# Lightning attention and a mish MLP on one core: attention outputs and scores on parts of the TensorE array

## The chip, the cores and the metric

The kernel runs on one core of a Trainium2 chip. The metric is the device time of one execution in microseconds (us); three runs of the kernel before gave a median of 219.52 us (219.44 to 220.08). A core has TensorE for matmuls (PE in the profile, its weight loads PEld), VectorE (DVE), ScalarE (ACT), GpSimd (POOL) and SyncE (SP), which issues transfers. TensorE reads its operands from SBUF and writes only to PSUM, a small memory of eight banks; VectorE and ScalarE bring results from there back to SBUF.

## The reference

Inputs are q, k, v of shape (4, 8, 768, 64), a decay lam per head, and the weights w_in (512, 2048) and w_out (2048, 512). Attention is linear attention with decay, in blocks along the sequence:

```python
for b in range(nb):
    intra = einsum('bhic,bhjc->bhij', qb, kb) * Dmask      # lam ** (i - j), i >= j
    intra = einsum('bhij,bhjd->bhid', intra, vb)
    inter = einsum('bhid,bhde->bhie', qb * lam_pow, kv_state)
    out[:, :, sl] = intra + inter
    kv_state = lam_block * kv_state + einsum('bhsd,bhse->bhde', kb_dec, vb)
```

The heads are then laid side by side, x of shape (3072, 512), and pass through an MLP: h = x @ w_in, g = h * tanh(softplus(h)), output g @ w_out in float32.

## The kernel before, in words

The sequence is cut into NG = 6 groups of C = 128 positions, n = 0 to 5 in the code (the first to the sixth group); a group holds these positions of all four batches, 512 tokens. For a group n, attention writes a transposed tile xt (features on partitions, tokens along the row). The first product of the MLP (mm1_unit, line 427) makes 16 blocks of 128 features of 512 tokens, each of four 128x512 matmuls, and ScalarE applies mish into hsg (line 434). The second product is a plain one for n = 0 (mm2_unit) and, in the others, a scheme of seven products with sums of weights and tokens (fast_unit, line 593), 14 units of eight matmuls of 256 columns (line 525), whose token sums gsum VectorE makes (line 498).

Attention of group n+1 is woven into the units of group n. In this text, stage n is the time in which the units of group n run. The work of a group's attention is cut into eight half-heads: a batch b and four of the eight heads (hf), that is two pairs of heads. Each half-head has three pieces, and att_pieces (line 397) lists them as att_a of half-head t, att_s of t-1, att_o of t-2. The loop over units at the end takes one or two pieces behind each unit, by a table (room). Each engine works its own queue in the order in which the program gives it the instructions.

- att_a (line 306): in the third to the sixth group (n >= NT = 2) q and k come already transposed by DMA, issued by SyncE in turn (line 263): qraw and kraw, k scaled by its decay on GpSimd or VectorE first (ktil, line 259). TensorE updates the state with att_kv (line 276: two 128-column matmuls of ktil and v into pv). VectorE multiplies qraw by its decay (qT, line 318) and copies kraw into kz (line 322): kz holds for each pair a tile in which only the 64 rows of one head are filled and the other 64 are zero, so that a matmul over all 128 rows gives one head's scores. VectorE adds state and pv (raw, line 298), GpSimd multiplies by the block decay (w, line 299). In the second group (n = 1) TensorE does the transposes and ScalarE fills kz (line 344).
- att_s (line 353): four 128x128 matmuls per half-head, kz stationary, qT moving, into one PSUM bank psS; from n = 2 on two banks, named pS and pk, are used in turn by successive half-heads. VectorE multiplies 512 columns by the causal mask into sb (line 362).
- att_o (line 365): for each pair, a matmul of the state w (128x128, the two heads as diagonal blocks) with qT, then two matmuls with sb, whose stationary operand is v in vz: a tile in which 64 columns of v alternate with 64 zero columns, so that 128 columns that start at a head's v give that head on the first 64 partitions and zero on the others, and 128 that start at the zeros ahead of the next head's v give that head on the last 64; the three matmuls of a pair accumulate in psO. ScalarE copies to xt (line 382).

The first group (n = 0) has no state and is done ahead of the loop: first_t transposes, first_s computes scores per head from 64 rows of the array, with the two heads of a pair in two banks (line 230), first_o the outputs with vz (line 244). TensorE is kept busy there with matmuls of zeros (busy, line 162). All loads of q, k, v, w_in (win) and w_out are issued by GpSimd; v goes into vz (line 80). vz has eight buffers and kz four; their zeros are written once by VectorE (lines 152, 700, 702).

Of the kernel before, what the change touches and what calls it, by code (L numbers as in the profile page):

```python
# [7 lines left out]
F32 = mybir.dt.float32  # L8
F16 = mybir.dt.float16
AF = mybir.ActivationFunctionType  # L10
ALU = mybir.AluOpType


def bc(ap, axis, n):
    shape = list(ap.shape)
    shape.insert(axis, n)
    return ap.unsqueeze(axis).broadcast_to(shape)
# [3 lines left out]
def kernel(  # L21
# [10 lines left out]
    nc = tc.nc  # L32
    B, H, S, D = q.shape
    C = 128
# [8 lines left out]
    NVB = 8  # L43
    NKB = 4
    NT = 2

    ctx.enter_context(tc.manual_schedule())
    const = ctx.enter_context(tc.tile_pool(name="const", bufs=1))
    loads = ctx.enter_context(tc.tile_pool(name="loads", bufs=NVB))
    work = ctx.enter_context(tc.tile_pool(name="work", bufs=2))  # L50
# [3 lines left out]
    kn = [None] * (NG * B)  # L54
    qn = [None] * (NG * B)

    vz = [const.tile([128, H, 2 * D], F16, name=f"vz{i}") for i in range(NVB)]

    def chunk_rows(t, i):
        n, b = divmod(i, B)  # L60
        return t[b, :, n * C : (n + 1) * C, :].rearrange("h p c -> p h c")
# [15 lines left out]
        nc.gpsimd.dma_start(out=qn[i], in_=chunk_rows(q, i))  # L77

    def load_v(i):
        nc.gpsimd.dma_start(out=vz[i % NVB][:, :, 0:D], in_=chunk_rows(v, i))  # L80

    WS = 4

# [64 lines left out]
    kzero = kzero2[:, 0:128]  # L148
    one1 = const.tile([1, 128], F32, name="one1")
    nc.vector.memset(one1, 1.0)  # L150
    for i in range(B):
        nc.vector.memset(vz[i][:, :, D : 2 * D], 0.0)
    kz = [const.tile([128, 2, 2, C], F16, name=f"kz{i}") for i in range(NKB)]
    nc.vector.tensor_scalar(out=ident, in0=rel, scalar1=0.0, scalar2=None, op0=ALU.is_equal)
    nc.vector.tensor_scalar(out=gone, in0=rel, scalar1=0.0, scalar2=-30000.0,
# [48 lines left out]
    sb0 = {}  # L204
# [31 lines left out]
    def first_o(c):  # L236
        if xt[0] is None:
            xt[0] = work.tile([128, JP, GT], F16, name="xt", tag="xt", bufs=2)
        psO = ps.tile([128, JP, C], F32, name="pO", tag="pO")
        vf = vz[c].rearrange("p h c -> p (h c)")  # L240
        for j in range(JP):
            for t in range(2):
                o = 4 * D * j + D * t
                nc.tensor.matmul(psO[:, j, :], vf[:, o : o + 128], sb0[c][t][:, j, :],
                                 start=(t == 0), stop=(t == 1))
        nc.scalar.activation(xt[0][:, :, c * C : (c + 1) * C], psO, AF.Copy)


# [27 lines left out]
    def att_kv(s, spare):  # L276

        n, b, hf = s.n, s.b, s.hf
        i = n * B + b
        pv = ps.tile([128, 2, 128], F32, name="pv", tag=spare, bufs=2)  # L280
        for p in range(2):
            j = 2 * hf + p
            nc.tensor.matmul(  # L283
                pv[:, p, :].rearrange("p (a e) -> p a e", a=2),
                ktil[i][:, 4 * hf + 2 * p : 4 * hf + 2 * p + 2, :].rearrange("p h c -> p (h c)"),
                vz[i % NVB][:, 2 * j : 2 * j + 2, 0:D], start=True, stop=True,
            )
        s.pv = pv

# [16 lines left out]
    def att_a(s):  # L306

        n, b, hf = s.n, s.b, s.hf
        i = n * B + b
        lqh = lq[:, 2 * hf : 2 * hf + 2, :]  # L310
        s.qT = work.tile([128, 2, C], F16, name="qT", tag="qT", bufs=5)
        s.kz = kz[s.seq % NKB]
        kp = [ktil[i][:, 4 * hf + 2 * p : 4 * hf + 2 * p + 2, :].rearrange("p h c -> p (h c)")
              for p in range(2)]
        if n >= NT:
            if n < NG - 1:
                att_kv(s, s.spare)
            nc.vector.tensor_tensor(  # L318
                out=s.qT, in0=qraw[i][:, 2 * hf : 2 * hf + 2, :], in1=lqh, op=ALU.mult)
            for hp in range(2):  # L320
                rs = slice(64 * hp, 64 * hp + 64)
                nc.vector.tensor_copy(s.kz[rs, :, hp, :], kraw[i][rs, 2 * hf : 2 * hf + 2, :])  # L322
            if n < NG - 1:
                att_w(s)
            if hf == 0 and i + 2 < s.loaded:
                turn(i + 2)
            if hf == 1 and i + B < NG * B:
                load_chunk(i + B)
            return
        pk = ps.tile([128, 2, C], F32, name="pk", tag="pk")  # L330
        pq = ps.tile([128, 2, C], F16, name="pq", tag="pq")
        for p in range(2):
            nc.tensor.matmul(pk[:, p, :], kp[p], ident, start=True, stop=True)
        for p in range(2):
            j = 2 * hf + p
            nc.tensor.matmul(
                pq[:, p, :], qn[i][:, 2 * j : 2 * j + 2, :].rearrange("p h c -> p (h c)"),
                ident, is_transpose=True, start=(p == 0), stop=(p == 1),
            )
        att_kv(s, s.spare)  # L340
        nc.vector.tensor_tensor(out=s.qT, in0=pq, in1=lqh, op=ALU.mult)
        for hp in range(2):
            rs = slice(64 * hp, 64 * hp + 64)
            nc.scalar.activation(s.kz[rs, :, hp, :], pk[rs], AF.Copy)
        if hf == 0 and i + 1 < s.loaded:
            scale_k(i + 1)
        elif hf == 0:
            turn(i + 1)
        att_w(s)
        if hf == 1:  # L350
            ahead.pop(0)()

    def att_s(s):

        psS = ps.tile([128, 4, C], F32, name="pS", tag=("pS", "pk")[s.seq % 2 if s.n >= NT else 0])
        for p in range(2):
            for hp in range(2):
                nc.tensor.matmul(  # L358
                    psS[:, 2 * p + hp, :], s.kz[:, p, hp, :], s.qT[:, p, :], start=True, stop=True,
                )  # L360
        s.sb = work.tile([128, 4, C], F16, name="sb", tag="sb", bufs=4)
        nc.vector.tensor_tensor(  # L362
            out=s.sb, in0=psS, in1=bc(maskT, 1, 4), op=ALU.mult)

    def att_o(s):

        n, b, hf = s.n, s.b, s.hf
        i = n * B + b
        if xt[n] is None:
            xt[n] = work.tile([128, JP, GT], F16, name="xt", tag="xt", bufs=2)  # L370
        psO = ps.tile([128, 2, C], F32, name="pO", tag=("pO", "pq")[s.seq % 2 if s.n >= NT else 0])
        vf = vz[i % NVB].rearrange("p h c -> p (h c)")
        for p in range(2):
            j = 2 * hf + p
            nc.tensor.matmul(psO[:, p, :], wst[b][hf][n % 2][:, p, :], s.qT[:, p, :],
                             start=True, stop=False)
            for hp in range(2):
                o = 4 * D * j + D * hp
                nc.tensor.matmul(psO[:, p, :], vf[:, o : o + 128], s.sb[:, 2 * p + hp, :],  # L379
                                 start=False, stop=(hp == 1))  # L380
        dst = xt[n][:, 2 * hf : 2 * hf + 2, b * C : (b + 1) * C]
        nc.scalar.activation(dst, psO, AF.Copy)  # L382

# [261 lines left out]
    for n in range(NG):  # L645
# [31 lines left out]
        for u, (fn, args) in enumerate(units):  # L677
            rest = fn(*args)
            if n == 0 and 19 <= u < 23:
                weight_sum(0 if u < 21 else 2, u % 2)  # L680
            if n == 1 and 4 <= u < 8:
                weight_sum(1 if u < 6 else 3, u % 2)
            if n > 0 and u in (9, 10):
                token_sum(n, 2, u - 9)
            if n > 0 and u == NKI - 3:
                token_sum(n, 0, 0)
            if n > 0 and u == NKI - 2:
                token_sum(n, 1, 0)
            if n > 0 and u == NKI - 1:
                token_sum(n, 0, 1)  # L690
                token_sum(n, 1, 1)
            if n > 0 and u in (NKI + 2, NKI + 3):
                token_sum(n, 3, u - NKI - 2)
            if n == 0 and 2 <= u < 2 + nh:
                att_kv(first_halves[u - 2], "po")
                att_w(first_halves[u - 2])
            if n == 0 and u % 2 == 1 and 0 < (u + 1) // 2 < B:
                scale_k((u + 1) // 2)
            if n == 0 and nh + 2 <= u < nh + 2 + NVB - B:
                nc.vector.memset(vz[u - nh - 2 + B][:, :, D : 2 * D], 0.0)  # L700
            if n == 0 and nh + 2 <= u < nh + 2 + NKB:
                nc.vector.memset(kz[u - nh - 2], 0.0)
            if n == 0 and u == 17:
                q_decays()
            if n == 0 and u == 16:
                nc.vector.tensor_scalar(out=maskT, in0=rel, scalar1=0.0, scalar2=None, op0=ALU.is_ge)
            if n == 0 and u == 18:
                scale_k(B)
            if n > 0 and pieces and u == 0:
                if n > 1:  # L710
                    turn((n + 1) * B)
                turn((n + 1) * B + 1)
            for _ in range(room.get(u, 0)):
                f2, s = pieces.pop(0)
                s.spare = "po" if u < NKI - 1 else "ph"
                f2(s)
            if n == 0 and rest:
                rest()
# [34 lines left out]
```

## Time and profile before

The profiled execution has a span of 217.4 us from its first to its last instruction; its own time is not among the three runs, whose median, 219.52 us, stands 2.1 us above that span.

| | before |
|---|---|
| median of 3 runs | 219.52 us (219.44 to 220.08) |
| span of the profiled execution | 217.4 us |
| TensorE busy | 204.8 us, 1672 matmuls |
| VectorE busy | 146.1 us, 309 instructions |
| ScalarE busy | 101.3 us |
| GpSimd busy | 116.6 us |
| granted TensorE clock | 1.000 |

A row of the profile names the line of the kernel, the engine, the operation, output and inputs, shapes and count; in the grouped view it then gives busy us in all, mean ns of one, the idle time before them, and what ended it. In the timeline a row begins with start and length in us, and a bracket at its end gives the engine's idle time just before and what released it. Matmuls are pipelined: one of 128 columns is shown with 0.22 us, though the next follows after about 0.055 us.

### The profile page before, as it was taken

How to read it: one execution, taken by the hardware profiler on the slowest of the kernel's cores; microseconds unless marked ns; L12 is line 12 of the kernel's file. 1: busy time of each engine (PE TensorE's matmuls, PEld its weight loads, DVE VectorE, ACT ScalarE, POOL GpSimd, SP SyncE). 2: the span in 40 equal slices, each digit the busy share in tenths (PEclk: the TensorE clock that was granted, in tenths of full speed). 3: DMA queues.
4: the chain of work that ended last, by engine and by line, in shares of the span. 5: the costliest groups of instructions: out<-in, count | busy, mean ns of one | idle time of the engine just before them, and what ended most of it. 6: DMA issues, size and time to landing. Idle time of an engine off the chain costs nothing.

```text
span 217.4 us, 4272 instructions
## 1 busy us (share of the span) xinstructions
PE 204.8 (94%) x1672; PEld 136.6 (63%) x1672; DVE 146.1 (67%) x309; ACT 101.3 (47%) x190; POOL 116.6 (54%) x139
## 2 busy tenths in 40 slices
PE   7899999999999799999979999979999999999993
PEld 2465544576545587745669845669845699644893
DVE  6667561877669999339999419999439987213433
ACT  5465566567665231166522176623166632266410
POOL 7996334998988768808757908757700002000020
PEclk9999999999999999999999999999999999999999
DMA  9999999999999999975999965999985201300014
GB/s 133 141 158 198 203 203 175 175 152 125 150 149 104 100 75 121 163 152 70 104 71 113 142 160 74 119 75 71 151 168 100 48 3 48 130 18 0 0 59 137
DMA packets 103766, 24.66 MB, mean 113 GB/s; under 512 B 93890, under 2 KB 103234, under 8 KB 103746
## 3 DMA queue, kind: packets, MB, share of 16 engines
q0 software_dynamic: 78080, 13.37, 80.3%
q1 hardware_dynamic: 22688, 8.39, 17.8%
q10 hardware_dynamic: 2978, 2.62, 4.0%
q8 instruction: 13, 0.21, 0.4%
q14 instruction: 7, 0.06, 0.1%
HBM read 27.26 MB, written 6.29 MB: 154 GB/s over the span
## 4 chain that ended last, share of the span: by engine, by line
PE 63%; DVE 20%; POOL 5%; issue 4%; DMA 4%; ACT 1%; ACTq 0%; POOLq 0%; DVEq 0%
PE ph L420 26%; PE z L525 10%; PE po L442 6%; PE y L525 6%; PE x L525 5%; DVE qT L318 5%; DVE kz L322 4%; DVE sb L362 4%; DVE gsum L498 4%; DMA win<-in_moe_w_in_dram 4%; PE pO L379 3%; DVE raw L298 3%; PE pS L358 2%; PE fin L525 2%; POOL vz L80 2%
## 5 line engine op out<-in xcount | busy, mean ns | idle before, releaser
L420 PE MATMUL ph<-xt,win 128*128 128x512 f16 (+2 forms) x404 | 89.6, 368 | 0.5 <-ACT hsg L434 0.2
L434 ACT ACTIVATE hsg<-ph 128x512 f16<-128x512 f32 x96 | 57.0, 597 | 45.6 <-PE ph L420 45.5
L420 PEld LDWEIGHTS <-win 128*128 128x128 f16 x404 | 37.0, 98 | 35.1 <-issue 0.6
L299 POOL TENSOR_TENSOR w<-raw,lbm 128x256 f16<-128x256 f32 x32 | 25.2, 791 | 29.0 <-DVE raw L298 28.9
L578 POOL TENSOR_TENSOR u<-u,p 128x512 f32<-128x512 f32 x5 | 6.5, 1293 | 52.0 <-DVE u L576 52.0
L525 PEld LDWEIGHTS <-gsum 128*128 128x128 f16 x336 | 30.8, 98 | 3.5 <-issue 0.5
L362 DVE TENSOR_TENSOR sb<-pS,maskT 128x512 f16<-128x512 f32 x40 | 27.2, 683 | 2.0 <-PE pS L358 1.9
L382 ACT ACTIVATE xt<-pO 128x256 f16<-128x256 f32 x40 | 15.2, 382 | 27.4 <-PE pO L379 27.2
L318 DVE TENSOR_TENSOR qT<-qraw,lq 128x256 f16<-128x256 f16 x32 | 19.1, 598 | 10.3 <-DMA qraw<-qn 10.3
L525 PEld LDWEIGHTS <-hsg 128*128 128x128 f16 x240 | 22.7, 98 | 2.5
L69 POOL DMA_DIRECT2D kn<-in_k_dram x23 | 21.4, 932 | 4.5 <-DMA win<-in_moe_w_in_dram 1.7
L80 POOL DMA_DIRECT2D vz<-in_v_dram x24 | 21.7, 906 | 3.3 <-DMA wout<-in_moe_w_out_dram 1.7
L77 POOL DMA_DIRECT2D qn<-in_q_dram x23 | 20.7, 898 | 5.1 <-DMA wout<-in_moe_w_out_dram 3.3
L498 DVE TENSOR_TENSOR gsum<-hsg 128x1024 f16<-128x1024 f16 x20 | 14.5, 725 | 12.9 <-ACT hsg L434 12.9
L322 DVE COPY kz<-kraw 64x256 f16<-64x256 f16 x64 | 19.9, 311 | 1.9 <-DMA kraw<-ktil 0.9
L379 PE MATMUL pO<-sb,vz 128*128 128x128 f16 x160 | 17.3, 219 | 3.6 <-DVE sb L362 3.2
L525 PE MATMUL z<-tsum,gsum 128*128 128x256 f16 x160 | 20.4, 272 | 0.2
L525 PE MATMUL x<-wout,hsg 128*128 128x256 f16 x160 | 20.1, 273 | 0.0
L358 PE MATMUL pS<-qT,kz 128*128 128x128 f16 x160 | 16.6, 220 | 1.8 <-DVE kz L322 1.6
L358 PEld LDWEIGHTS <-kz 128*128 128x128 f16 x160 | 11.8, 98 | 7.8 <-DVE kz L322 3.0
L298 DVE TENSOR_TENSOR raw<-pv,w 128x256 f32<-128x256 f32 x32 | 13.5, 422 | 4.1 <-PE pv L283 3.4
L379 PEld LDWEIGHTS <-vz 128*128 128x128 f16 x160 | 12.6, 98 | 5.7 <-issue 4.9
(89 smaller groups left out, 242.8 us busy)
## 6 DMA issues: line engine op xcount, KB each, us to landing
out_dram<-osum SPq DMA_DIRECT2D x14, 256.0 KB, 3.2
vz<-in_v_dram POOLq DMA_DIRECT2D x24, 128.0 KB, 4.7
kn<-in_k_dram POOLq DMA_DIRECT2D x23, 128.0 KB, 4.4
qn<-in_q_dram POOLq DMA_DIRECT2D x23, 128.0 KB, 4.6
wout<-in_moe_w_out_dram POOLq DMA_DIRECT2D x4, 512.0 KB, 16.5
win<-in_moe_w_in_dram POOLq DMA_DIRECT2D x3, 512.0 KB, 10.1
out_dram<-osum ACTq DMA_DIRECT2D x5, 256.0 KB, 4.0
out_dram<-osb ACTq DMA_DIRECT2D x4, 256.0 KB, 5.5
```

What stands on the lines that cost most here:

```text
L69: nc.gpsimd.dma_start(out=kn[i], in_=chunk_rows(k, i))
L80: nc.gpsimd.dma_start(out=vz[i % NVB][:, :, 0:D], in_=chunk_rows(v, i))
L299: nc.gpsimd.tensor_tensor(out=w_new, in0=raw, in1=lb, op=ALU.mult)
L318: nc.vector.tensor_tensor(out=s.qT, in0=qraw[i][:, 2 * hf : 2 * hf + 2, :], in1=lqh, op=ALU.mult)
L322: nc.vector.tensor_copy(s.kz[rs, :, hp, :], kraw[i][rs, 2 * hf : 2 * hf + 2, :])
L358: nc.tensor.matmul(psS[:, 2 * p + hp, :], s.kz[:, p, hp, :], s.qT[:, p, :], start=True, stop=True,)
L362: nc.vector.tensor_tensor(out=s.sb, in0=psS, in1=bc(maskT, 1, 4), op=ALU.mult)
L379: nc.tensor.matmul(psO[:, p, :], vf[:, o : o + 128], s.sb[:, 2 * p + hp, :], start=False, stop=(hp == 1))
L420: nc.tensor.matmul(ph_t[ni][:, lo:hi], win0[min(ni, 2)][:, kc, max(ni - 2, 0) * 128 : max(ni - 2, 0) * 128 + 128] if ni < w else win[ni // ...
L434: nc.scalar.activation(hsg[n][:, ni, :], ph_t.pop(ni), AF.Mish)
L498: nc.vector.tensor_tensor(out=gsum[n, i][:, ks, :], in0=a, in1=b, op=op)
L525: nc.tensor.matmul(t, lhs(kk, b), rhs(kk, c, c + w), start=(fresh and kk == 0 and (alone or i == 0)), stop=(kk == HK - 1), skip_group_chec ...
```

## The change

v is loaded without zero columns (vd in place of vz). In the outputs of all groups each head's matmul with sb has 64 stationary columns and writes its own 64 partitions of psO; the two heads of a pair differ in the half of the array's columns that they use. The state matmuls keep 128 columns and now both come first. In the groups n = 2 to 5 the scores are taken from kraw itself: 64 rows of it and of qT for each head, one head of a pair into the bank pS and the other into pk, and the mask is multiplied in two operations of 256 columns, one for each bank. The copies into kz go in these groups (they stay for n = 1), and so do the memsets of vz.

```diff
-    vz = [const.tile([128, H, 2 * D], F16, name=f"vz{i}") for i in range(NVB)]
+    vd = [const.tile([128, H, D], F16, name=f"vd{i}") for i in range(NVB)]
...
-        nc.gpsimd.dma_start(out=vz[i % NVB][:, :, 0:D], in_=chunk_rows(v, i))
+        nc.gpsimd.dma_start(out=vd[i % NVB], in_=chunk_rows(v, i))
...
-    for i in range(B):
-        nc.vector.memset(vz[i][:, :, D : 2 * D], 0.0)
...
-        vf = vz[c].rearrange("p h c -> p (h c)")
         for j in range(JP):
             for t in range(2):
-                o = 4 * D * j + D * t
-                nc.tensor.matmul(psO[:, j, :], vf[:, o : o + 128], sb0[c][t][:, j, :],
-                                 start=(t == 0), stop=(t == 1))
+                nc.tensor.matmul(psO[64 * t : 64 * t + 64, j, :], vd[c][:, 2 * j + t, :],
+                                 sb0[c][t][:, j, :], start=True, stop=True)
...
-                vz[i % NVB][:, 2 * j : 2 * j + 2, 0:D], start=True, stop=True,
+                vd[i % NVB][:, 2 * j : 2 * j + 2, :], start=True, stop=True,
...
-            for hp in range(2):
-                rs = slice(64 * hp, 64 * hp + 64)
-                nc.vector.tensor_copy(s.kz[rs, :, hp, :], kraw[i][rs, 2 * hf : 2 * hf + 2, :])
...
-        psS = ps.tile([128, 4, C], F32, name="pS", tag=("pS", "pk")[s.seq % 2 if s.n >= NT else 0])
+        if s.n >= NT:
+            i = s.n * B + s.b
+            t = [ps.tile([128, 2, C], F32, name="pS", tag=tag) for tag in ("pS", "pk")]
+            for p in range(2):
+                for hp in range(2):
+                    rs = slice(64 * hp, 64 * hp + 64)
+                    nc.tensor.matmul(t[hp][:, p, :], kraw[i][rs, 2 * s.hf + p, :], s.qT[rs, p, :],
+                                     start=True, stop=True)
+            s.sb = work.tile([128, 2, 2, C], F16, name="sb", tag="sb", bufs=4)
+            for hp in range(2):
+                nc.vector.tensor_tensor(
+                    out=s.sb[:, hp], in0=t[hp], in1=bc(maskT, 1, 2), op=ALU.mult)
+            return
+        psS = ps.tile([128, 4, C], F32, name="pS", tag="pS")
...
-        vf = vz[i % NVB].rearrange("p h c -> p (h c)")
         for p in range(2):
-            j = 2 * hf + p
             nc.tensor.matmul(psO[:, p, :], wst[b][hf][n % 2][:, p, :], s.qT[:, p, :],
-                             start=True, stop=False)
+                             start=(p == 0), stop=False, skip_group_check=True)
+        for p in range(2):
             for hp in range(2):
-                o = 4 * D * j + D * hp
-                nc.tensor.matmul(psO[:, p, :], vf[:, o : o + 128], s.sb[:, 2 * p + hp, :],
-                                 start=False, stop=(hp == 1))
+                nc.tensor.matmul(psO[64 * hp : 64 * hp + 64, p, :],
+                                 vd[i % NVB][:, 4 * hf + 2 * p + hp, :],
+                                 s.sb[:, hp, p, :] if n >= NT else s.sb[:, 2 * p + hp, :],
+                                 start=False, stop=True, skip_group_check=True)
...
-            if n == 0 and nh + 2 <= u < nh + 2 + NVB - B:
-                nc.vector.memset(vz[u - nh - 2 + B][:, :, D : 2 * D], 0.0)
```

## The prediction

> **What bounds the kernel now.** I read the page first, then busy time by stretch, then the chain of waits and single stretches of the timeline.
>
> ```profile
> span 217.4 us, 4272 instructions
> ...
> PE 204.8 (94%) x1672; PEld 136.6 (63%) x1672; DVE 146.1 (67%) x309; ACT 101.3 (47%) x190; POOL 116.6 (54%) x139
> ...
> PE 63%; DVE 20%; POOL 5%; issue 4%; DMA 4%; ACT 1%; ACTq 0%; POOLq 0%; DVEq 0%
> ```
>
> TensorE is busy nearly all the time and carries 63% of the chain that ended last, yet VectorE carries 20%. To see where, I cut the span at the group borders. Stage n works on the MLP of group n and on the attention of group n+1; the rows are stages 1 to 4 (start, end and length, then busy us of each engine with its instructions).
>
> ```profile
> core 0: us, PE busy (x) PEld busy (x) DVE busy (x) ACT busy (x) POOL busy (x), PEclk, DMA share, GB/s
> 57.00:90.60 33.60, 30.96 (x261) 21.68 (x261) 26.41 (x52) 13.22 (x26) 27.93 (x32) 1.00 1.49 115
> 90.60:124.00 33.40, 31.98 (x274) 22.65 (x272) 25.52 (x52) 14.21 (x27) 22.20 (x27) 1.00 1.05 112
> 124.00:157.40 33.40, 31.97 (x274) 22.65 (x272) 25.54 (x52) 14.21 (x27) 21.15 (x24) 1.00 1.04 111
> 157.40:188.00 30.60, 30.60 (x258) 21.67 (x256) 21.49 (x48) 14.17 (x27) 1.27 (x1) 1.00 0.36 76
> ```
>
> The granted clock is 1.00 throughout. A busy TensorE here includes the tails of pipelined matmuls, so I count its work by the pace at which matmuls follow each other, from the chain:
>
> ```profile
> 170.88 1.73 PE ph L420 x8
> 172.61 0.22 PE pS L358 x4
> 173.17 1.75 PE x L525 x16
> ```
>
> That is 0.055 us for 128 columns, 0.216 for 512 and 0.109 for 256. Stage 2 issues 64 matmuls of 512 columns (13.8 us), 112 of 256 (12.25) and 8 half-heads' worth of 12 attention matmuls of 128 (96, 5.3): 31.4 of its 33.4 us, so 2.0 are lost to waiting; stage 3 is the same. Stage 4 has no state update, 16 matmuls fewer: 30.5 of 30.6, nothing is lost. In stage 1 a part of the first three feature blocks was done before it began: 13 whole blocks (52 matmuls of 512, 11.2), about 0.5 of remainders, then 12.25 and 5.3: 29.2 of 33.6, 4.4 lost. Together 8.5 us of waiting, and the timeline shows for what:
>
> ```profile
> 70.48 2.05 DVE L318 TENSOR_TENSOR qT<-qraw,lq 128x256 f16<-128x256 f16 x1
> ...
> 71.16 1.08 POOL L259 TENSOR_TENSOR ktil<-kn,lk 128x512 f16<-128x512 f16 x1
> ...
> 72.72 0.60 PE L358 MATMUL pS<-qT,kz 128*128 128x128 f16 x4 [1.19 <-DVE kz L322]
> ...
> 108.84 0.48 PE L358 MATMUL pS<-qT,kz 128*128 128x128 f16 x4
> ...
> 111.04 0.68 DVE L362 TENSOR_TENSOR sb<-pS,maskT 128x512 f16<-128x512 f32 x1
> ...
> 111.77 0.27 PE L379 MATMUL pO<-sb,vz 128*128 128x128 f16 x2 [1.24 <-DVE sb L362]
> ```
>
> TensorE waits in its queue for kz and sb, both late because VectorE runs behind: at 70.48 it even stood still over qT, 2.05 us, while GpSimd worked on ktil. So stages 1 to 3 end by VectorE's lag in their middle, stage 4 by TensorE alone.
>
> **The change part by part.** VectorE first.
>
> ```profile
> L322 DVE COPY kz<-kraw 64x256 f16<-64x256 f16 x64 | 19.9, 311 | 1.9 <-DMA kraw<-ktil 0.9
> L362 DVE TENSOR_TENSOR sb<-pS,maskT 128x512 f16<-128x512 f32 x40 | 27.2, 683 | 2.0 <-PE pS L358 1.9
> L152 DVE MEMSET vz<- 128x256 uint32 x4 | 1.1, 272 | 0.0
> L700 DVE MEMSET vz<- 128x256 uint32 x4 | 1.1, 272 | 0.0
> ```
> ```profile
> 111.97 0.47 DVE L322 COPY kz<-kraw 64x256 f16<-64x256 f16 x2
> 112.47 0.42 DVE L298 TENSOR_TENSOR raw<-pv,w 128x256 f32<-128x256 f32 x1
> 112.81 0.68 DVE L362 TENSOR_TENSOR sb<-pS,maskT 128x512 f16<-128x512 f32 x1
> 113.41 0.84 DVE L498 TENSOR_TENSOR gsum<-hsg,gsum 128x1024 f16<-128x1024 f16 x1
> ```
>
> All 64 copies of k into the zeroed halves go: 0.50 us per half-head undisturbed (111.97 to 112.47), 2 x 0.311 = 0.62 on average with stalls. The mask becomes two operations of 256 columns; the nearest row is raw, also 256 columns out of PSUM, which holds VectorE for 0.34 (112.47 to 112.81), against 0.60 for one of 512 (112.81 to 113.41): +0.08. So VectorE loses 0.42 to 0.54 per half-head, 3.4 to 4.3 us per stage, against 2.0 (stages 2, 3) and 4.4 (stage 1) of waiting. What is late next there is the mask behind the two or four gsum operations, which wait for the last mish; I leave 0.3 in stages 2 and 3 and 0.6 in stage 1. TensorE gets back 8.4 - 1.2 = 7.2 us. The bounds are 0 and 8.5.
>
> The vz memsets cost nothing: four (1.1 us) lie in the start, where the path is the load of win, four in stage 0, where TensorE sets the pace. If that cover were gone they would be a gain of at most 1.1.
>
> ```profile
> 21.13 0.55 PEld L420 LDWEIGHTS <-win 128*128 128x128 f16 x4 [0.28 <-DMA win<-in_moe_w_in_dram]
> L80 POOL DMA_DIRECT2D vz<-in_v_dram x24 | 21.7, 906 | 3.3 <-DMA wout<-in_moe_w_out_dram 1.7 <-DMA win<-in_moe_w_in_dram 1.6
> L77 POOL DMA_DIRECT2D qn<-in_q_dram x23 | 20.7, 898 | 5.1 <-DMA wout<-in_moe_w_out_dram 3.3 <-DMA win<-in_moe_w_in_dram 1.7
> ```
>
> The v loads now fill dense tiles as the q loads do; 906 against 898 ns an issue is nothing. The kraw buffer is freed by the score matmuls instead of the copies, some 1 us later, with four buffers: nothing.
>
> Now TensorE. Only one place in this trace tiles the array, the 64-row scores of group n = 0:
>
> ```profile
> 15.14 0.38 PE L162 MATMUL busy<-kzero 128*128 128x512 f16 x1
> 15.45 0.40 PE L230 MATMUL pS<-pqT,pkT 64*128 64x128 f16 x8
> ```
> ```profile
> 15.45 0.23 PEld L230 LDWEIGHTS <-pkT 64*128 64x128 f16 x8 [0.26 <-ACT pkT L218]
> 15.78 0.31 PEld L420 LDWEIGHTS <-win 128*128 128x128 f16 x2
> ```
>
> Eight 64-row matmuls hold the array for 0.33 us (15.45 to 15.78), less than 8 x 0.055 = 0.44: the two heads of a pair do run together. But four pairs should need 0.22, so leaving the mode costs 0.11. And the 512-column matmul of 15.14 is through at 15.36 while the first tiled load starts at 15.45: entering costs 0.09. A visit to a tiled mode is thus 0.20 plus 0.055 a pair. (At the other row-tiled visits TensorE came in idle, so the entry rests on this one.)
>
> Scores, 32 half-heads: two pairs, 0.31 in place of 4 x 0.055 = 0.22, so +0.09. Attention outputs, 40 half-heads: the two state matmuls keep their 128 columns and are followed by two pairs on 64 columns. No trace shows a 64-column mode. Upper bound: pairs don't overlap and each of four loads of 98 ns lies open, 0.20 + 0.39 = 0.59 against 0.22, +0.37. Lower bound: no cost of switching, 0.11 against 0.22, -0.11. I take the row-tiled visit, the nearest row, plus 0.03 for a first weight load that stands open: +0.12.
>
> Stages 1 to 4: 32 x (0.09 + 0.12) = +6.7. Stage 0, the outputs of group n = 1 alone: 8 x 0.12 = 1.0, hidden between not at all and wholly in the waits at its end; I take 0.3 of it as hidden: +0.7. First outputs, of group n = 0: 0.20 + 4 x 0.055 + 0.03 = 0.45 in place of 0.44, and ahead of the win load anyway: 0. Sum: +6.7 + 0.7 - 7.2 = +0.2. The profiled span becomes 217.6; the median of the runs, 219.52, stands 2.1 above the span, so 219.7. By stage: stage 4 about 30.6 + 1.7 = 32.3, stages 2 and 3 about 33.4 each, stage 1 about 31.5.
>
> **The rivals.**
>
> Slower, by the weight loads of the column tiles. TensorE hides a 128-column load behind a matmul because it can be drawn ahead; a load row lasts 98 ns:
>
> ```profile
> L379 PEld LDWEIGHTS <-vz 128*128 128x128 f16 x160 | 12.6, 98 | 5.7 <-issue 4.9
> ```
>
> If a pair on 64 columns goes at the 98 ns of a load instead of 55, each half-head's two pairs cost 0.09 more: 40 x 0.09 = +3.6, 223.3. It decides from an output visit of +0.14 per half-head on (0.02 over mine, 40 times, is 0.3%). For it: nothing in the trace has a 64-column load. Against it: in the row-tiled visit eight loads took 0.23 us. The Trainium skill speaks for it: "TensorEngine Tiling (Array Packing)", Restrictions, says that column tiling disables fast weight load, and "TensorE: Matmul & The Clock Gate", LDWEIGHTS, gives columns / 1.2 ns for a plain load. By that estimate 64 columns take 53 ns: hidden if both tiles load at once, and about 107 a pair if one after the other, which would make 40 x 0.1 = +4. No run here shows it. Chance 0.18.
>
> Slower, by the banks. Each half-head now takes both score banks, so its scores wait for the mask of the half-head before, where the old kernel had another bank free. TensorE works in order, so the outputs of the half-head before and the next MLP matmuls stand behind such a wait, and ScalarE behind them. In the rows above the scores at 108.84 went ahead though the mask of the half-head before began at 111.04; under the new rule they would have waited until 111.72, 2.9 us, in place of the 1.4 us that the outputs lost. If VectorE stays that late (gsum and qT stalled behind GpSimd, like the 2.05 above, instead of kz), half of the 7.2 is not won: 223.3. Against it: without the copies the mask comes some 2 us earlier by then. It decides when a mask ends later than one half-head's period, about 3 us, after its scores. Chance 0.10.
>
> Faster, by cheap column switches. If going between 128 and 64 columns doesn't empty the array, as rows do not prove that it must, the outputs cost between -0.11 and +0.12 per half-head; half way 40 x 0.115 = 4.6 us less: 215.1. Against it stands only the likeness to the 0.09 and 0.11 of rows. "TensorEngine Tiling", Key Properties, says that any change of tiling mode drains the array, which would leave this rival nothing. Chance 0.22.
>
> **How the numbers follow.** My case has 0.50: 219.7, and by 0.03 per half-head of switching and 1 us of waiting left or won, 218.1 to 221.3 for itself. A measurement tells 0.3%, 0.66 us, from no change. Within my case I give faster 0.32, same 0.42, slower 0.26, as its centre lies within that band. With the rivals: faster 0.16 + 0.22 = 0.38; same 0.21; slower 0.13 + 0.28 = 0.41. Cases of both signs hold most of it. The range takes the centres of all rivals with some of their spread: 215.0 to 224.0; beyond lie the far halves of the column bounds.
>
> **What would show it.** Stage 4, which loses nothing to VectorE now, shows the bare price: about 32.3 us if right, 30.6 or less if column switches are cheap, over 33 if loads are open. In stages 1 to 3 the waits of 1.19 for kz and 1.24 for sb should be gone and VectorE near 22 us in stages 2 and 3 (25.5 less 3.4 to 4.3); a wait of TensorE at the scores for sb would show the bank rival. The start of the weight loads after the last output matmul of a half-head gives the column visit directly: 0.11 after it for the row-like exit. I am wrong if stage 4 doesn't grow, or if stages 2 and 3 keep over 1 us of waiting.

## The result and the profile after

The changed kernel takes 223.1 us as a median of four runs (221.85 to 223.66), the kernel before 219.49 beside it: the ratio is 1.0141 (95% interval 1.0099 to 1.0184), slower by more than the 0.3% that a measurement can tell. The forecast was 219.7 us in a range of 215.0 to 224.0; the time lies in the range, and above the 218.1 to 221.3 that the forecast gave for its own case. The profiled execution of the changed kernel has a span of 221.6 us against 217.4.

The page of the changed kernel, busy time by engine and the chain by engine:

```profile
span 221.6 us, 4233 instructions
...
PE 211.9 (96%) x1672; PEld 127.9 (58%) x1672; DVE 129.9 (59%) x269; ACT 101.6 (46%) x190; POOL 117.0 (53%) x139
...
PE 84%; DVE 9%; issue 2%; DMA 2%; ACT 1%; ACTq 0%; DVEq 0%
```

VectorE gave up 16 us of work (146.1 to 129.9) and more than half of its part of the chain (20% to 9%). TensorE took the chain over (63% to 84%), with as many matmuls and 7 us more of busy time. Cut into stages 1 to 4, each from the first 512-column matmul of one group's MLP to that of the next:

```profile
59.17:91.53 32.36, 30.83 (x261) 19.57 (x261) 22.80 (x43) 13.12 (x26) 28.24 (x32) 1.00 1.56 123
91.53:125.48 33.95, 33.39 (x275) 20.58 (x272) 21.43 (x44) 14.31 (x27) 22.67 (x26) 1.00 1.04 111
125.48:159.43 33.95, 33.39 (x275) 20.57 (x272) 21.42 (x44) 14.31 (x27) 20.43 (x23) 1.00 1.02 109
159.43:192.00 32.57, 32.45 (x259) 19.61 (x257) 18.85 (x40) 14.32 (x27) 1.26 (x1) 1.00 0.27 66
```

By the same cut the kernel before has 33.5, 33.4, 33.4 and 30.5. So stage 1 is 1.1 us shorter, stages 2 and 3 are 0.55 longer each and stage 4 is 2.06 longer. Stage 0 (from the first 512-column matmul of the second MLP product) went from 24.8 to 25.5. Those add up to 2.7 us; the profiled spans differ by 4.2. The other 1.5 us lie in the start, ahead of everything that the forecast spoke of.

Three places carry the explanation. First, a visit to the tiled modes in stage 4, on TensorE and on its weight loads (start and length, a few instructions merged in a row):

```profile
169.35 0.28 PE L354 MATMUL pS<-qT,kraw 64*128 64x128 f16 x4
169.56 0.28 PE L379 MATMUL pO<-qT,w 128*128 128x128 f16 x2
169.78 0.30 PE L383 MATMUL pO<-sb,vd 128*64 128x128 f16 x4
170.01 0.39 PE L426 MATMUL ph<-xt,win 128*128 128x512 f16 x1
```
```profile
169.34 0.11 PEld L354 LDWEIGHTS <-kraw 64*128 64x128 f16 x4 [0.42 <-issue]
169.56 0.11 PEld L379 LDWEIGHTS <-w 128*128 128x128 f16 x2
169.78 0.14 PEld L383 LDWEIGHTS <-vd 128*64 128x64 f16 x4
170.01 0.11 PEld L426 LDWEIGHTS <-win 128*128 128x128 f16 x2
```

Two state matmuls need 0.11 at the pace of 0.055, but the four matmuls on 64 columns behind them begin 0.22 after them (169.56 to 169.78): 0.11 more than the matmuls are worth. Two pairs on 64 columns also need 0.11, but the next MLP matmul begins 0.23 after them, 0.12 more. At each of these borders the first weight loads start together with the matmuls of their mode and not before, while in the kernel before the load for the matmul of zeros at 15.14 starts at 15.09. The four loads on 64 columns took 0.14 us together, with 0.11 for the four on 64 rows. A longer visit, in the outputs of the first group, shows the pairs themselves:

```profile
16.77 0.41 PE L240 MATMUL pO<-sb,vd 128*64 128x128 f16 x8
17.11 0.39 PE L160 MATMUL busy<-kzero 128*128 128x512 f16 x1
```

Four pairs with the way out of the mode take 0.34 us (16.77 to 17.11); less 0.1 for the way out that is 0.06 for a pair.

Second, the scores in stage 2, on VectorE and on TensorE:

```profile
108.60 0.89 DVE L504 TENSOR_TENSOR gsum<-hsg 128x1024 f16<-128x1024 f16 x1 [0.46 <-ACT hsg L440]
109.53 1.10 DVE L504 TENSOR_TENSOR gsum<-gsum,hsg 128x1024 f16<-128x1024 f16 x1
110.55 0.74 DVE L358 TENSOR_TENSOR sb<-pS,maskT 128x256 f16<-128x256 f32 x2
```
```profile
109.75 0.82 PE L531 MATMUL x<-wout,hsg 128*128 128x256 f16 x6
111.01 0.60 PE L354 MATMUL pS<-qT,kraw 64*128 64x128 f16 x4 [0.45 <-DVE sb L358]
```

The old waits for kz and for sb in the outputs are gone, and a new one stands in their place: the scores of a half-head wait for the mask of the one before (110.55 to 111.29), because each half-head now fills both banks. That mask stands in VectorE's queue behind two token sums, and the first of these waits for the last mish. TensorE stands for 0.6 us ahead of these scores (six matmuls from 109.75 on are through at 110.40), and 0.27 more between the two heads, as the second bank is freed later than the first: 0.87 us, of which 0.1 is the change of mode that was due in any case. So this wait costs about 0.8 us, once in stage 2 and once in stage 3.

Third, the same in stage 1, where TensorE stands for 1.58 us ahead of the scores and 0.27 between the heads, 1.85 together and 1.75 without the change of mode. On VectorE, on TensorE and on GpSimd:

```profile
70.96 1.80 DVE L314 TENSOR_TENSOR qT<-qraw,lq 128x256 f16<-128x256 f16 x1
72.68 0.41 DVE L294 TENSOR_TENSOR raw<-pv,w 128x256 f32<-128x256 f32 x1
73.02 1.87 DVE L504 TENSOR_TENSOR gsum<-gsum,hsg 128x1024 f16<-128x1024 f16 x1
74.81 0.74 DVE L358 TENSOR_TENSOR sb<-pS,maskT 128x256 f16<-128x256 f32 x2
```
```profile
75.28 0.60 PE L354 MATMUL pS<-qT,kraw 64*128 64x128 f16 x4 [1.41 <-DVE sb L358]
```
```profile
71.70 0.77 POOL L295 TENSOR_TENSOR w<-raw,lbm 128x256 f16<-128x256 f32 x1
72.38 1.27 POOL L255 TENSOR_TENSOR ktil<-kn,lk 128x512 f16<-128x512 f16 x1
73.62 0.71 POOL L295 TENSOR_TENSOR w<-raw,lbm 128x256 f16<-128x256 f32 x1
```

qT takes 0.41 us elsewhere and 1.80 here, the sum 0.68 elsewhere and 1.87 here. Each ends some tenths of a us after a GpSimd operation has ended, a little less than the time that it takes alone: qT at 72.76, 0.29 after the first w (72.47), the sum at 74.89, 0.56 after the second (74.33).

### The profile page after: what moved, and what is told of

Same layout as the page of the kernel before. It is cut to its first block, busy times and chain, and to the rows that moved or that the text cites. A ratio compares the mean times of both kernels' runs of the same rounds, so it can differ in the third digit from the quotient of the medians.

```text
span 221.6 us, 4233 instructions
## 1 busy us (share of the span) xinstructions
PE 211.9 (96%) x1672; PEld 127.9 (58%) x1672; DVE 129.9 (59%) x269; ACT 101.6 (46%) x190; POOL 117.0 (53%) x139
## 4 chain that ended last, share of the span: by engine, by line
PE 84%; DVE 9%; issue 2%; DMA 2%; ACT 1%; ACTq 0%; DVEq 0%
PE ph L426 35%; PE z L531 13%; PE y L531 7%; PE po L448 6%; PE x L531 5%; PE pO L383 4%; DVE gsum L504 3%; PE pS L354 3%; PE pO L379 2%; DVE sb L358 2%; DMA qn<-in_q_dram 2%; PE pv L279 2%; DVE qT L314 2%; PE fin L531 2%; PE busy L160 1%
## 5 line engine op out<-in xcount | busy, mean ns | idle before, releaser
L531 PEld LDWEIGHTS <-gsum 128*128 128x128 f16 x336 | 29.9, 98 | 4.9
L358 DVE TENSOR_TENSOR sb<-pS,maskT 128x256 f16<-128x256 f32 x64 | 23.9, 413 | 9.5 <-PE pS L354 9.5
L504 DVE TENSOR_TENSOR gsum<-hsg 128x1024 f16<-128x1024 f16 x20 | 16.4, 821 | 15.0 <-ACT hsg L440 15.0
L69 POOL DMA_DIRECT2D kn<-in_k_dram x23 | 21.4, 930 | 4.4 <-DMA win<-in_moe_w_in_dram 1.7
L80 POOL DMA_DIRECT2D vd<-in_v_dram x24 | 21.7, 904 | 3.9 <-DMA win<-in_moe_w_in_dram 2.2
L314 DVE TENSOR_TENSOR qT<-qraw,lq 128x256 f16<-128x256 f16 x32 | 17.8, 556 | 7.7 <-DMA qraw<-qn 7.7
L255 POOL TENSOR_TENSOR ktil<-kn,lk 128x512 f16<-128x512 f16 x15 | 16.6, 1116 | 0.1
L448 PE MATMUL po<-wout,hsg 128*128 128x512 f16 x64 | 15.2, 380 | 0.0
L354 PE MATMUL pS<-qT,kraw 64*128 64x128 f16 x128 | 9.9, 221 | 2.8 <-DVE sb L358 2.3
L383 PE MATMUL pO<-sb,vd 128*64 128x128 f16 x160 | 12.1, 231 | 0.0
L354 PEld LDWEIGHTS <-kraw 64*128 64x128 f16 x128 | 4.3, 94 | 12.9 <-issue 12.5
```

Source lines behind the costliest of these rows:

```text
L69: nc.gpsimd.dma_start(out=kn[i], in_=chunk_rows(k, i))
L80: nc.gpsimd.dma_start(out=vd[i % NVB], in_=chunk_rows(v, i))
L314: nc.vector.tensor_tensor(out=s.qT, in0=qraw[i][:, 2 * hf : 2 * hf + 2, :], in1=lqh, op=ALU.mult)
L354: nc.tensor.matmul(t[hp][:, p, :], kraw[i][rs, 2 * s.hf + p, :], s.qT[rs, p, :], start=True, stop=True)
L358: nc.vector.tensor_tensor(out=s.sb[:, hp], in0=t[hp], in1=bc(maskT, 1, 2), op=ALU.mult)
L383: nc.tensor.matmul(psO[64 * hp : 64 * hp + 64, p, :], vd[i % NVB][:, 4 * hf + 2 * p + hp, :], s.sb[:, hp, p, :] if n >= NT else s.sb[:, 2 ...
```

## The experiments

The theory after the result has three parts: each change of mode costs about 0.095 us wherever it is; the scores' new wait is one of queue order on VectorE; and the start is a matter of when the clock comes. The rivals: the price lies in the 64-column loads or in the scores' two banks, VectorE is late by its load whatever the order, and the start's new form is slow. Where stage lengths are given below, each is cut as above; they repeat within 0.02 us from kernel to kernel where the code of a stage is the same.

**One half of the change alone: outputs on 64 columns.** The kernel before, with dense v and

```diff
-                nc.tensor.matmul(psO[:, p, :], vf[:, o : o + 128], s.sb[:, 2 * p + hp, :],
-                                 start=False, stop=(hp == 1))
+                nc.tensor.matmul(psO[64 * hp : 64 * hp + 64, p, :],
+                                 vd[i % NVB][:, 4 * hf + 2 * p + hp, :], s.sb[:, 2 * p + hp, :],
+                                 start=False, stop=True, skip_group_check=True)
```

> The old kernel with only the outputs changed: 64 columns a head and dense v in all groups; scores, kz copies and masks stay as they were. Theory (switching): the changed kernel's trace shows about 0.095 us of idle array at each entry and exit of a tiled mode, so an output visit costs 0.095 + 0.095 + 0.02 + 2 x 0.056 = 0.32 in place of 0.22, +0.1 per half-head. Stage 4, which waits for nobody, goes from 30.5 to 31.3 us; in stages 1 to 3 a part hides behind VectorE's lag. In all +2 to +4 us, 221.5 to 223.5. Rival (the loss comes from the scores and their banks): stage 4 stays at 30.5 and the time within 0.5 us of the kernel before.

Measured: 222.32 us, ratio 1.0127 (1.0082 to 1.0172). Stage 4 has 31.43 us, 0.92 more than before, 0.115 per half-head; stages 2 and 3 have 33.83 (before 33.4), since VectorE's lag, with its copies in place, covers the other half there: TensorE's waits in stage 2, counted from the gaps between its matmuls, fall from 2.0 to 1.5 us. The outputs lose on their own; the rival falls.

**The other half alone: scores on 64 rows.** The changed kernel with vz, its memsets and the old outputs.

> The changed kernel with the old outputs: padded v on 128 columns and its memsets everywhere; scores on 64 rows, two banks, no kz copies. Theory (switching): half of the switches go, 8 x 0.1 = 0.8 us in each of stages 1 to 4 against the changed kernel; stage 4 at 31.2 to 31.7 (before 30.5, changed 32.6), stages 2 and 3 at 33.1 to 33.4; with the start of the kernel before, 217.5 to 219.5 in all. Rival (bank waits and VectorE's lag hold stages 1 to 3): what TensorE no longer needs turns into longer waits at the scores, stages 2 and 3 stay at 33.8 to 34.0, and the time is 219.5 to 221.

Measured: 221.74 us, ratio 1.0056 (1.0007 to 1.0105). Stages 2 and 3 have 33.4, 0.57 less than the changed kernel, as the theory has it, and the wait at the scores grew from 0.87 to 1.22 us, which is the rival's part: both held. Stage 4 has 31.76. The total is above what I expected, by its start and by stage 1. There the wait for the mask is 1.65 us long, and behind it the clock fell:

```profile
75.00:77.00 2.00, 1.62 (x18) 1.31 (x18) 1.97 (x5) 0.13 (x1) 1.97 (x3) 0.98 1.34 123
77.00:80.30 3.30, 3.30 (x22) 2.17 (x20) 1.19 (x4) 0.74 (x2) 0.72 (x1) 0.50 1.41 90
80.30:85.00 4.70, 4.70 (x53) 4.05 (x52) 4.05 (x11) 1.85 (x4) 2.54 (x4) 1.00 0.04 5
```

The column behind POOL is the granted clock: 0.50 for some 3.4 us. Its stage 1 took 33.24 us, 0.9 more than that of the changed kernel, though it has half the switches.

**The start.** The changed kernel, with padded v, memsets and 128-column outputs for the first group alone:

```diff
     vd = [const.tile([128, H, D], F16, name=f"vd{i}") for i in range(NVB)]
+    vz = [const.tile([128, H, 2 * D], F16, name=f"vz{i}") for i in range(B)]
...
+    for i in range(B):
+        nc.vector.memset(vz[i][:, :, D : 2 * D], 0.0)
...
```

> The changed kernel, but the outputs of the first group as before: four padded v tiles with their memsets at the start, 128 columns. Theory A (the start's new form delays the full clock): in the changed kernel's records the full clock is granted at 15.2 us, in those of the kernel before at 10.4; with the old start it comes at about 10 us again and the time falls by 1.5 to 2 us, to 221.1 to 221.6. Theory B (the grant moves by itself): the grant comes at either time, and the runs spread between 221.5 and 223.7 as those of the changed kernel do.

Measured: 223.03 us, ratio 1.0146 (1.0101 to 1.0191); the stages are those of the changed kernel, and the profiled start was as late as there. Theory B. The pace shows when the clock came: the transposes of the third chunk in the kernel before, then in the changed kernel.

```profile
11.68 0.39 PE L212 MATMUL pk<-ident,kn 128*128 128x128 f16 x4
11.90 0.39 PE L212 MATMUL pq<-ident,qn 128*128 128x128 f16 x4
```
```profile
13.11 0.63 PE L210 MATMUL pk<-ident,kn 128*128 128x128 f16 x4
13.53 0.63 PE L210 MATMUL pq<-ident,qn 128*128 128x128 f16 x4
```

Four matmuls of 128 columns follow each other in 0.22 us in the one and in 0.42 in the other: half the pace. In the profiles' records of the clock, full speed was granted at 10.4 us in the kernel before and 15.2 us in the changed one, and in ten experiments anywhere between 9.4 and 15.9 us. (Ahead of its first record the clock column of a profile reads 1.00 as well, so that the pace is the better witness there.) The form of the start doesn't decide it: three kernels with the new first outputs (outputs alone, sums behind, and scores of a batch with outputs on columns) had the grant at 9.5 to 11.1 us, and both rows-only kernels, with the old ones, at 15.5 and 15.6. In these twelve profiles the first MLP matmul starts at 16.0 to 16.5 us where it came by 11.1 and at 17.8 to 18.5 where it came after 14.6. Beside eight of the experiments the kernel before itself ran between 218.69 and 222.37 us, 34 runs. So up to 2 us of any pair of single profiles is this, and of the 4.2 us between the two profiled spans 1.5 are.

**A fuller start.** The changed kernel with the sums moved (next paragraph) and four matmuls of zeros more where TensorE stood idle:

```diff
-    busy(1)
+    busy(3)
     first_s(0)
...
     first_t(1)
+    busy(2)
```

> The changed kernel with the sums behind, and four matmuls of zeros more in the start, two ahead of the first scores and two behind the second transposes, where TensorE sat idle for 0.75 and 0.76 to 1.2 us. Theory (the clock is granted after some microseconds of unbroken work, and the idle stretches of the start make it miss): the grant, seen at 9.5 to 15.5 us in six profiles, comes by 10 us, and the runs spread less than the 219.6 to 222.8 of the kernel with the sums behind. Rival (the grant moves by itself): grant and spread stay as they are, or the added matmuls only cost their time.

Measured: 220.61 us, 219.86 to 222.71 in ten runs, against 220.28, 219.55 to 222.78, without: no effect on median or spread; the profiled grant came at 12.2 us. The theory that idle stretches in the start make it miss the clock is not borne out. Nor is all of the spread the start's: in both kernels the two longest runs have a mean granted clock of 0.992, the others 0.997 to 1.000. One stretch of 3.4 us at half clock, as in the rows-only kernel, would give 0.992 (1.7 of 220 us lost).

**The order of VectorE's queue.** The changed kernel with the two last token sums behind the attention pieces of their unit:

```diff
-            if n > 0 and u == NKI - 1:
-                token_sum(n, 0, 1)
-                token_sum(n, 1, 1)
...
             for _ in range(room.get(u, 0)):
                 f2, s = pieces.pop(0)
                 s.spare = "po" if u < NKI - 1 else "ph"
                 f2(s)
+            if n > 0 and u == NKI - 1:
+                token_sum(n, 0, 1)
+                token_sum(n, 1, 1)
```

> The changed kernel, with the two last token sums (behind the 16th MLP unit of a stage) handed to VectorE after that unit's attention pieces instead of before them. Theory (bank wait): in stages 2 and 3 the changed kernel's scores at 111.0 wait 0.6 + 0.27 us for a mask that stands behind these two sums; with the mask ahead of them the wait goes and each of the two stages shortens from 33.95 to about 33.1, the time by 1.5 to 2 us. Rival (VectorE is simply late there, whatever the order): the wait moves to the next scores or to the products of the sums, and the stages stay within 0.2 us of 33.95.

Measured: 220.28 us, ratio 1.0012 (0.9972 to 1.0053). Its stages 2 to 4:

```profile
90.12:123.25 33.13, 33.13 (x274) 20.39 (x272) 21.43 (x44) 14.30 (x27) 22.20 (x26) 1.00 1.04 114
123.25:156.38 33.13, 33.13 (x274) 20.42 (x272) 21.42 (x44) 14.30 (x27) 19.95 (x23) 1.00 1.03 112
156.38:188.61 32.23, 32.23 (x258) 19.51 (x256) 18.87 (x40) 14.30 (x27) 1.27 (x1) 1.00 0.27 67
```

33.13 as expected, and TensorE is busy for all of it; VectorE's work is the same 21.4 us. Stage 4 lost 0.34 us of waiting too. It was order, not load.

**GpSimd's hold on VectorE.** The same, with the scalings of k that fall into stage 1 on VectorE:

```diff
-        (nc.vector if i <= B or i >= (NG - 1) * B else nc.gpsimd).tensor_tensor(
+        (nc.vector if i <= B or 2 * B < i < 3 * B or i >= (NG - 1) * B else nc.gpsimd).tensor_tensor(
```

> The changed kernel with the sums behind, and the three scalings of k that stage 1 takes on GpSimd (chunks 9 to 11) moved to VectorE, 0.69 us each. Theory (GpSimd's operations hold up those of VectorE that read two SBUF tensors: in stage 1 a qT of 1.80 and a gsum of 1.87 us, and behind them the mask for which the scores wait 1.58 + 0.27 us): with GpSimd idle the two stalls and the wait go, and stage 1 falls from 32.4 to about 31 us. Rival (VectorE has too much work in stage 1): with 2 us more of it the wait at the scores stays or grows, stage 1 at 32.4 or more.

Measured: stage 1 fell from 32.36 to 31.32 us though VectorE has 1.1 us more to do there:

```profile
59.12:90.44 31.32, 31.03 (x260) 19.68 (x260) 23.94 (x50) 13.11 (x26) 24.83 (x29) 1.00 1.64 126
```

```profile
71.57 0.41 DVE L314 TENSOR_TENSOR qT<-qraw,lq 128x256 f16<-128x256 f16 x1
72.24 1.56 DVE L504 TENSOR_TENSOR gsum<-gsum,hsg 128x1024 f16<-128x1024 f16 x1
```
```profile
71.80 1.45 POOL L295 TENSOR_TENSOR w<-raw,lbm 128x256 f16<-128x256 f32 x2
```

The qT of 1.80 is at 0.41 again; a sum still takes 1.56 us beside two w operations of GpSimd, and ends 0.55 after the second of them. The Trainium skill says as much: in "SBUF — State Buffer", Who interferes with whom, a VectorE instruction with two SBUF inputs contends with a GpSimd instruction that reads SBUF, for ports that only one of them holds at a time. The trace agrees, and it shows that two GpSimd operations without a gap between them hold one VectorE operation through both. (220.27 us in its single run.)

**Twice the switches.** The changed kernel with the outputs of each pair finished in turn:

```diff
         for p in range(2):
             nc.tensor.matmul(psO[:, p, :], wst[b][hf][n % 2][:, p, :], s.qT[:, p, :],
                              start=(p == 0), stop=False, skip_group_check=True)
-        for p in range(2):
             for hp in range(2):
```

> The changed kernel with the outputs of each pair finished in turn: state matmul, its two 64-column matmuls, then the next pair, so that each half-head's outputs go into the tiled mode and out of it twice; the matmuls are the same. Theory (0.095 us at each switch, whatever is done between): two switches more per half-head, 16 per stage, +1.5 us; stage 4 from 32.6 to 34.1, stages 2 and 3 from 33.95 to about 35.4, the whole some 6 to 7 us more. Rival (the price is that of the 64-column loads, not of the switch): nothing is loaded more often, stage 4 stays near 32.6.

Measured: 231.08 us in its single run, span 229.3. Stages 2 and 4:

```profile
94.89:130.24 35.35, 35.22 (x275) 21.47 (x273) 21.28 (x44) 14.40 (x27) 21.95 (x25) 1.00 0.96 105
165.58:199.74 34.16, 34.16 (x259) 20.52 (x256) 18.86 (x40) 14.41 (x27) 1.27 (x1) 1.00 0.25 63
```

Stage 4 grew by 1.59 us for 16 switches, 0.10 each, with the same matmuls and loads. But the changed kernel's stage 4 has 0.34 us of the wait for the mask, and this one, by the gaps between its matmuls, less than 0.1: against the 32.23 of the kernel with the sums moved it is 1.93, 0.12 each, as at the two sides above. The price is the switch's, with the load that stands open behind it. The whole grew by 7.75 us against the changed kernel's profiled run, more than the 6 to 7 expected, as stage 0 took 1.4 us more too.

**Fewer switches.** First the rows-only kernel with the sums behind:

> Scores on 64 rows with the old 128-column outputs (the rows-only kernel), and the two last token sums behind the attention pieces. Theory (switches cost 0.1 each, and the mask behind the sums 0.85 per stage): stages 2 and 3 fall from 33.4 to about 32.5, stage 4 stays at 31.5 to 31.8; against the kernel before 1 to 2 us less. Rival (VectorE limits stages 2 and 3 once TensorE has less to do): they stay above 33.1.

Measured: 218.75 us, ratio 0.9929 (0.9894 to 0.9964). Stages 2 and 3 have 32.21, stage 4 31.31; stage 1 keeps its 33.23 with the halved clock. Then the scores of a whole batch in one visit, in this kernel and in the changed one:

```diff
+            if s.hf == 0:
+                return
+            i = s.n * B + s.b
+            t = [ps.tile([128, 4, C], F32, name="pS", tag=tag) for tag in ("pS", "pk")]
+            for j in range(JP):
+                h = s if j >= 2 else s.mate
+                for hp in range(2):
+                    rs = slice(64 * hp, 64 * hp + 64)
+                    nc.tensor.matmul(t[hp][:, j, :], kraw[i][rs, j, :], h.qT[rs, j % 2, :],
+                                     start=True, stop=True)
+            both = [work.tile([128, 4, C], F16, name="sb", tag="sb", bufs=4) for hp in range(2)]
+            for hp in range(2):
+                nc.vector.tensor_tensor(out=both[hp], in0=t[hp], in1=bc(maskT, 1, 4), op=ALU.mult)
...
```

The outputs follow one step later. With the old outputs:

> The same with the scores of both half-heads of a batch taken in one visit: four pairs of 64-row matmuls into the same two banks (four heads' 128 columns each), two masks of 512 columns per batch, the outputs one step later. Theory (price per visit, not per matmul): four visits fewer per stage at 0.2 us, so stage 4 goes from about 31.6 to 30.8, stages 2 and 3 to 31.7 to 32.0; VectorE also gains 0.08 us per half-head; in all 2 to 3 us under the kernel before. Rival (the masks now come in lumps and the outputs wait for them): stage 4 at 31.5 or more, waits at the outputs.

With outputs on 64 columns:

> The changed kernel (outputs on 64 columns) with the sums behind and the scores of a batch in one visit. Theory: against the kernel with the sums behind alone, 0.8 us less per stage (four visits of 0.2): stage 4 from 32.2 to about 31.4, stages 2 and 3 from 33.1 to 32.3; the outputs' own switches, 16 x 0.095 per stage, remain and keep it 0.7 to 0.9 us per stage behind the kernel with old outputs. Rival (outputs on columns gain something once the scores are out of the way): no difference per stage to the kernel with old outputs.

Measured: 214.96 us with the old outputs, ratio 0.9788 (0.9724 to 0.9851), and 217.16 on columns, 0.9874 (0.982 to 0.9927). Stages 1 to 4 of the former:

```profile
57.23:88.61 31.38, 29.56 (x261) 20.43 (x260) 22.06 (x35) 13.40 (x26) 29.70 (x32) 1.00 1.66 129
88.61:120.65 32.04, 31.69 (x274) 21.45 (x272) 22.73 (x36) 14.10 (x27) 22.83 (x25) 1.00 1.06 116
120.65:152.69 32.04, 31.69 (x274) 21.46 (x272) 22.73 (x36) 14.09 (x27) 20.84 (x23) 1.00 1.07 116
152.69:183.15 30.46, 30.46 (x258) 20.45 (x256) 18.09 (x32) 14.10 (x27) 1.27 (x1) 1.00 0.28 71
```

Stage 4 is at 30.46, 0.85 less than with a visit per half-head and level with the kernel before, whose full-array scores it replaces without any copy. Stages 2 and 3 keep 0.7 us of waits of the outputs for the masks, the lumps of the rival, and gain only 0.17. The whole is 4.8 us under the kernel before, where 2 to 3 were expected: stage 1 fell by 1.85 us, from 33.23 to 31.38, and its clock is 1.00 now, which the expectation had not counted on. On columns stage 4 has 31.39, 0.93 more: the outputs' switches, as in the first experiment. This kernel with the scores of a batch in one visit and outputs on the full array beats both kernels of this case.

## Why the prediction was right or wrong

- *The price of a visit: right.* 0.20 for entry and exit, taken from a single row of the first group, with 0.03 for an open load. That row could have misled, since its loads had also just been released by ScalarE (the 0.26 in its bracket); but the changed kernel's way into the scores, where nothing is waited for, takes 0.10 as well (the two MLP matmuls from 168.82 on are through at 169.25, the scores start at 169.35), and the outputs have 0.11 and 0.12 for the two sides with the open load in them. Predicted per half-head were 0.21 for scores and outputs together, 1.7 us for stage 4; without the waits that were taken away by moving the sums it has 32.23 - 30.51 = 1.72.
- *The column mode: right as likened to rows.* It was the unknown with the widest bounds, -0.11 to +0.37 per half-head; 0.115 was measured against 0.12. The rival of the loads falls: four 64-column loads start within 0.03 us, as pairs, and took 108 ns each against 93 to 98 for the others, and the four pairs of the first group follow each other at 0.06 us. The Trainium skill's rule ("TensorEngine Tiling (Array Packing)", Restrictions) that column tiling disables fast weight load may hold, but what the forecast worked out for its rival, 107 ns for each pair, is not seen. The rival of cheap column switches falls too; the Trainium skill's rule ("TensorEngine Tiling (Array Packing)", Key Properties) that a change of mode drains the array agrees with the trace, which has 0.1 us at each.
- *Stage 0: right*, +0.63 against +0.7.
- *What VectorE gives back: the step that failed.* The prediction left 0.3 us of waiting in stages 2 and 3 and 0.6 in stage 1; there were 0.8 and 1.75, and 0.3 in stage 4 where none was expected, 2.4 us more in all. It named the mechanism as its bank rival, with 0.10, and the sign that it gave for it, a wait of TensorE at the scores for sb, is what the rows show; the waits for kz and at the outputs are gone, as it said. (The 0.8 is under the 1 us that it had set as a sign of being wrong, and was still half a us too much in each stage.) It saw that the masks stand behind the token sums, but took for granted that without the copies they would come in time. In stages 2 and 3 they don't since the sums wait for ScalarE first, which no relief of VectorE hastens; in stage 1 since GpSimd holds VectorE. Moving two sums took away 0.82 in each stage, moving the scalings 1.04 in stage 1.
- *The start: not foreseen.* It was given no change. The first MLP matmul came 1.9 us later, as the clock did; by the third experiment and the grants of the other profiles, the new form of the start isn't what decides that. The prediction set its sum against one profiled start without asking how much a start varies. Whether the changed kernel's four runs, all above 221.8, drew late clocks by chance, or something in it makes a late one likelier, these runs don't settle: the kernel with the sums moved, the same but for these, ran at 219.55 at its fastest, 2.3 under the changed kernel's fastest, of which the sums explain 2.0.

Together: 4.2 us between the spans is 0.2 foreseen, 2.4 of waits and 1.5 of the start. That the time lies in the range is in part luck. The upper end was set by two rivals, both at 223.3: the one of the loads isn't seen, and the one of the banks came with 2.4 of its 3.6 us. Without the late start the changed kernel's profiled run would be at about 221.8, just above the forecast's own case.

## What to carry to other kernels

Count the visits to a tiled mode, not the matmuls in it: here a visit costs about 0.2 us of idle time, as much as four full matmuls of 128 columns, so two pairs in one lose and four pairs break even (shown for rows, by stage 4 at 30.46 against 30.51). When an engine is relieved of work, look at what its queue still holds ahead of the operation that others wait for, above all an operation that waits itself. And before a change of one per cent is judged, see how far the kernel that it is measured against moves by itself.

## What the runs showed of the hardware that was not expected

- Loads and matmuls of two tiles that lie side by side go together in both directions; only the change of mode takes time, 0.1 us each way, for rows and columns alike.
- Full clock came between 9.4 and 15.9 us after the start in twelve profiles of nearly the same start, worth about 2 us in all. A wait of 1.65 us on TensorE in stage 1 of the rows-only kernel was followed by 3.4 us at half clock; the wait of 1.41 us in the same place of the changed kernel was not. Cut from the grant on into stretches of 3.41 us, the length of the fall, the profiles show a border: two stretches, one in each of the rows-only kernels, have 2.15 and 2.09 us of gaps between TensorE's matmuls, and these alone were followed by half clock; no other in the twelve profiles has more than 1.96.
- A VectorE operation of 0.41 us on two SBUF operands took 1.80 us beside GpSimd's.
